# Sixteen idle matmuls before and inside the second norm of a decode block

## The chip, the cores and the metric

The kernel runs on one core of a Trainium2 chip, as one program. The metric is device time in microseconds (us) of one execution. The engines named below are PE (TensorE, the matrix engine; PEld is its weight load), DVE (VectorE), ACT (ScalarE), POOL (GpSimd) and SP (SyncE, whose queue issues nearly all transfers here). A matmul writes to PSUM, the accumulation memory, in banks of 512 columns.

## The reference

One transformer block in float32 for two sequences of one new token each: norm with a modulation from `c`, attention of 32 heads over a cache of 4096 keys and values, a second norm with modulation, and a dense layer pair with Mish between them.

```python
mod = (_silu(c) @ w_mod).reshape(c.shape[0], 6, 1, -1)
sa, ca, ga, sb, cb, gb = (mod[:, 0], mod[:, 1], mod[:, 2], mod[:, 3], mod[:, 4], mod[:, 5])
h = _layernorm(x, axis=-1) * (1 + ca) + sa
x = x + ga * _A_ref(h, A_k_cache, A_v_cache, A_wq, A_wo)   # softmax attention, 32 heads of 128
h = _layernorm(x, axis=-1) * (1 + cb) + sb
x = x + gb * _B_ref(h, B_w1, B_b1, B_w2)                   # 512 -> 1376, Mish, -> 512
```

Keys and values are 2 x 32 x 4096 x 128 floats each, so nearly everything that is read is cache: 297 MB in all, each byte used once.

## The kernel before, in words

All inputs are packed on the host into 36 loads, which go one after another through three rooms in SBUF (`load`, L142 to L155); a room is loaded again when what lay in it has been used (`used`, L159). SP issues the loads in their order and waits, ahead of a load, for the engine that still reads the room. The last load (m3 and w1, then m5 and w2: modulation 3, the first dense layer, a part of modulation 5, the second dense layer) is cut into seven transfers; its first waits for the end of head 30's V on PE, since the room it goes to held the values of heads 29 and 30.

Per head, DVE multiplies the keys by the query (L334) and sums (L337), PE brings the maxima together (L346), ACT takes the exponentials into `e_t` (L353), and PE multiplies them with the values: `weighted_v` (L371 to L382, the matmul is L375), 16 products of 512 columns for a head, each 32 columns of the array wide, four side by side. The program order of each engine is written by hand; nothing is moved by a scheduler.

After the last head's softmax comes the tail, where this change lies. In order on PE: V of heads 29 and 30 into the PSUM tile `ov[1]` (L488 to L490); the copy of it and its products with the denominators, `head_values` (L398, `otp`); `project_o` (L406, `att`); V of head 31 into `ov[0]` (L498); the folding of the attention output (L502, `xps`); `busy(1)`; head 31's `otp`; modulation 4 (L263) around the last head's output projection (L414). Then the second norm, `centred` and `rstd`: DVE sums, PE takes the mean over partitions (L226, `mean_b`), DVE subtracts and squares, PE takes the variance (L234, `var_b`), ACT and DVE make the reciprocal root. Modulation 3 (L263) waits for the last load's first piece; DVE joins both to `hq` (L543), PE turns it (L253, `h2ps`), DVE copies it to `h2t`, and the first dense layer follows (L554, `w1ps`, 16 products of up to 384 columns). Then Mish on ACT and DVE, and the second dense layer (L598, `yps`, 44 products), whose last products need the last pieces of the last load. Two sums on DVE and the store end the kernel.

Modulation 5 (`modulation_5`, L519 to L526, matmul L523) is put in pieces into gaps of this chain. Its first five terms have 20 rows each (`rows5`, padding to spread transfers), the next three 128 rows, the last 28; each term is four products of 128 columns, accumulated in `gps`, a part of `ov[0]`. `centred` takes a function `between` that is called after the squares and before the variance.

`busy(n)` (L310 to L314) computes nothing that is used: for `n` counts of 128 columns it multiplies the exponentials of another head with the unit matrix, 256 columns at a time, into `ov[1]`, which is free then. Such a product is called idle here.

## Time and profile before

| | |
|---|---|
| median of 3 runs | 697.68 us (697.03 to 698.01) |
| profiled execution | 696.76 us, its span 695.0 us |
| DVE busy | 588.2 us, 85% of the span |
| PE busy | 282.6 us, 41% |
| ACT busy | 44.2 us, 6% |
| HBM read | 297.17 MB, 428 GB/s over the span |
| load queue (q1) | 99.1% of 16 DMA engines |
| mean granted clock of TensorE | 0.671 |

The span runs from the first to the last instruction that the profiler recorded; the execution's time has a little around it. In the rows below, `L375` is a line of the kernel, `ov<-room,e` are the tiles written and read, `128*32` the rows and columns of the array that a matmul uses, `128x512` its output, `x32` a count. A matmul in float32 stands in the trace as two records, one per pass. In brackets stands how long the engine was idle ahead of it and what ended that. "PEclk" is the share of its full clock that TensorE was granted.

### The profile page before, as it was taken

Reading aid. Unit: us, or ns where it says so; the run is one execution under the profiler, and the core shown is the slowest. Engines: PE = TensorE matmul, PEld = TensorE weight load, DVE = VectorE, ACT = ScalarE, POOL = GpSimd, SP = SyncE. Lnnn points to the kernel's source line nnn. Section 1 sums busy time; section 2 is a strip of 40 time slices with the busy share of each in tenths; the row PEclk is TensorE's granted clock in tenths of the full one; section 3 lists DMA queues with packets and bytes.
Section 4 is the critical chain, followed back from the end, with each engine's and each line's share of the span. In section 5 each row is a group of like instructions: output and inputs, shape, how many; then the busy total and the mean of one; then the engine's idle time right before and its main releaser. Section 6 shows DMA issues by size and latency. Waiting matters only on the chain.

```text
span 695.0 us, 3978 instructions
## 1 busy us (share of the span) xinstructions
PE 282.6 (41%) x1664; PEld 102.0 (15%) x1664; DVE 588.2 (85%) x223; ACT 44.2 (6%) x169; POOL 4.4 (1%) x20
## 2 busy tenths in 40 slices
PE   2503334335145515335232705134343526124677
PEld 1201001001001201102100301011110101001235
DVE  3699899999999999999999989999999999899002
ACT  1000000000000000000000000000000010000011
POOL 2000000000000000000000000000000000000000
PEclk9755666668556665656585757666576657555789
DMA  9999999999999999999999999999999999999997
GB/s 378 464 426 422 423 445 453 420 426 430 422 457 434 427 430 427 438 441 427 426 441 426 450 426 426 430 435 438 438 426 424 445 430 446 426 421 425 429 419 303
DMA packets 6986, 297.49 MB, mean 428 GB/s; under 512 B 924, under 2 KB 1060, under 8 KB 1444
## 3 DMA queue, kind: packets, MB, share of 16 engines
q1 hardware_dynamic: 6808, 297.22, 99.1%
q8 instruction: 13, 0.21, 0.1%
q10 hardware_dynamic: 160, 0.02, 0.0%
q14 instruction: 5, 0.04, 0.0%
HBM read 297.17 MB, written 0.07 MB: 428 GB/s over the span
## 4 chain that ended last, share of the span: by engine, by line
DMA 67%; DVE 28%; PE 4%; issue 0%; ACT 0%; SPq 0%; DVEq 0%; ACTq 0%
DMA room<-in_load 67%; DVE room L334 14%; DVE s L337 14%; PE qps L307 1%; PE ov L375 1%; PE modps L263 1%; PE w1ps L554 1%; PE yps L598 0%; PE ov L523 0%; PE fps L569 0%; DVE m L350 0%; DVE hcw L296 0%; PE ov L314 0%; ACT q L308 0%; SPq L151 0%
## 5 line engine op out<-in xcount | busy, mean ns | idle before, releaser
L334 DVE TENSOR_TENSOR room<-room,q 128x8192 f32<-128x8192 f32 x32 | 278.1, 8692 | 46.4 <-DMA room<-in_load 40.3
L337 DVE TENSOR_REDUCE s<-room 128x64 f32<-128x8192 f32 x32 | 277.9, 8683 | 0.4 <-DVE m L350 0.3
L375 PE MATMUL ov<-room,e 128*32 128x512 f32 x1024 | 173.5, 829 | 77.2 <-ACT e L353 52.3
L346 PE MATMUL mt<-d,same 128*128 128x64 f32 x64 | 18.2, 379 | 199.7 <-DVE d L344 199.7
L375 PEld LDWEIGHTS ov<-room,e 128*32 128x32 f32 x1024 | 38.6, 143 | 183.2 <-issue 129.3
L353 ACT ACTIVATE e<-s,m 64x64 f32<-64x64 f32 x64 | 22.1, 345 | 554.2 <-DVE m L350 553.4
L346 PEld LDWEIGHTS mt<-d,same 128*128 128x128 f32 x64 | 13.1, 255 | 229.0 <-DVE d L344 182.0
L307 PE MATMUL qps<-room,hcw 128*128 128x512 f32 x64 | 44.4, 862 | 4.8 <-DMA room<-in_load 4.0
L361 PE MATMUL l<-l,ones 128*128 128x8 f32 x16 | 4.6, 358 | 75.4 <-ACT e L353 75.4
L398 PE MATMUL otp<-pick,o 128*128 128x8 f32 (+2 forms) x72 | 13.6, 316 | 33.6 <-ACT o L390 31.6
L307 PEld LDWEIGHTS qps<-room,hcw 128*128 128x128 f32 x64 | 17.1, 279 | 27.2 <-issue 21.3
L398 PEld LDWEIGHTS otp<-pick,o 128*128 128x128 f32 x72 | 12.8, 267 | 42.8 <-ACT o L390 39.8
L390 DVE COPY o<-ov 128x256 f32<-128x256 f32 x1 | 0.4, 425 | 21.8 <-ACT o L390 21.8
L361 PEld LDWEIGHTS l<-l,ones 128*128 128x128 f32 x16 | 3.8, 296 | 76.8 <-ACT e L353 76.8
L350 DVE TENSOR_REDUCE m<-mt 128x1 f32<-128x64 f32 x32 | 6.9, 217 | 7.6 <-PE mt L346 7.6
L406 PE MATMUL att<-room,ot 128*32 128x512 f32 x62 | 10.2, 719 | 5.2 <-DMA room<-in_load 4.7
L353 ACT ACTIVATION_READ_ACCUMULATOR e<-s,m 64x1 f32 x64 | 11.8, 185 | 0.0
L344 DVE TENSOR_SCALAR d<-half,m 128x64 f32<-128x64 f32 x32 | 8.1, 254 | 1.1
L342 DVE TENSOR_REDUCE m<-s 128x1 f32<-128x64 f32 x32 | 7.0, 217 | 0.9
L263 PE MATMUL modps<-room,ct 128*32 128x128 f32 (+1 forms) x128 | 6.8, 358 | 2.0 <-DMA room<-in_load 2.0
L390 ACT COPY o<-ov 128x512 f32<-128x512 f32 (+1 forms) x9 | 5.1, 561 | 25.4 <-PE ov L375 25.2
L308 ACT ACTIVATE q<-qps 128x512 f32<-128x512 f32 x8 | 4.8, 597 | 14.8 <-PE qps L307 14.6
(107 smaller groups left out, 63.1 us busy)
## 6 DMA issues: line engine op xcount, KB each, us to landing
room<-in_load SPq DMA_DIRECT2D x4, 4096.0 KB, 25.2
room<-in_load SPq DMA_DIRECT2D x1, 7168.0 KB
room<-in_load SPq DMA_DIRECT2D x1, 3072.0 KB, 26.1
room<-in_load SPq DMA_DIRECT2D x3, 1024.0 KB, 28.2
room<-in_load SPq DMA_DIRECT2D x1, 2400.0 KB, 13.1
room<-in_load SPq DMA_DIRECT2D x1, 1376.0 KB, 14.5
room<-in_load SPq DMA_DIRECT2D x1, 1280.0 KB, 15.1
room<-in_load SPq DMA_DIRECT2D x1, 768.0 KB
```

Of the source, the lines that this page charges most:

```text
L263: nc.tensor.matmul(ps[R * g : R * (g + 1)], lhsT=ct[:, k, :], rhs=t[:, k, :].rearrange("p (m n) -> p m n", m=n)[:, :, P * g : P * (g + 1)] ...
L307: nc.tensor.matmul(ps, lhsT=hcw[:, k, :], rhs=wq_t[ch][:, k, :], start=(k == 0), stop=(k == G - 1))
L334: nc.vector.tensor_tensor(out=k_t[h], in0=k_t[h], in1=qv, op=ALU.mult)
L337: nc.vector.tensor_reduce(out=s_t[h], in_=k_t[h], axis=AX.X, op=ALU.add)
L342: nc.vector.tensor_reduce(out=m_t[h][:, 0:1], in_=s_t[h], axis=AX.X, op=ALU.max)
L344: nc.vector.tensor_scalar(out=d, in0=half, scalar1=m_t[h][:, 0:1], scalar2=None, op0=ALU.mult)
L346: nc.tensor.matmul(mps[h], lhsT=same, rhs=d, start=True, stop=True)
L353: nc.scalar.activation(e_t[i][own_b, :, M * i + 4 * b : M * i + 4 * b + 4], s_t[h][own_b].rearrange("p (c m) -> p c m", m=4), AF.Exp, bias ...
L361: nc.tensor.matmul(lps[n], lhsT=ones, rhs=sum_t[n % 2], start=True, stop=True)
L375: nc.tensor.matmul(ov[bank][R * g : R * (g + 1), :], lhsT=e_t[h % HC][:, NB // 2 * part + c, :], rhs=v_t[h, part][:, c, :], start=(first a ...
L398: nc.tensor.matmul(tps[:, x], lhsT=o_t[m], rhs=pick_t[n][:, m, x], start=(m == 0), stop=(m == 3),)
L406: nc.tensor.matmul(att[R * i : R * (i + 1), :], lhsT=ot_t[n % 2][:, i, :], rhs=wo_t[n][:, i, :], start=(n == 0), stop=(n == H // HC - (2 i ...
```

## The change

`busy` gets the PSUM bank as an argument. Twelve idle products of 256 columns are put between head 29's V and head 30's, into `ov[0]`. In the second norm, two pieces of modulation 5 move ahead of the mean; three counts of idle columns (one product of 256, one of 128) take the place of the pieces between mean and variance; one idle product and two pieces follow modulation 3, where one piece stood; one idle product goes ahead of the last of these pieces, after `h2ps`. The sum of the pieces stays the same and so does their order among each other.

```diff
-    def busy(n):
+    def busy(n, bank=1):
...
-            nc.tensor.matmul(ov[1][:, :cols], lhsT=ident, ...
+            nc.tensor.matmul(ov[bank][:, :cols], lhsT=ident, ...
...
     for h in range(H - 3, H - 1):
+        if h == H - 2:
+            busy(24, 1 - N % 2)
         for part in range(2):
             weighted_v(h, part, N % 2, False, h == H - 2)
...
+    modulation_5(0, 2)
+
     xg = work.tile([P, P], F32, tag="sq", name="xg", bufs=1)
...
-    xc, var, rs = centred(x2, "b", add_x, lambda: modulation_5(0, 3))
+    xc, var, rs = centred(x2, "b", add_x, lambda: busy(3))
     mps3 = modulation("3", 1, wm3)
-    modulation_5(3, 4)
+    busy(1)
+    modulation_5(2, 4)
...
+    busy(1)
     modulation_5(4, PIECES)
```

PE's row before, from the sum of the denominators (`l`) to the end of head 30's V (`ov_110` is `ov[1]`, `ov_109` is `ov[0]`, `room_1196` holds the values of heads 29 and 30, `e_161` and `e_162` are their exponentials):

```order
L361 MATMUL l_1291<-l_167,ones 128x8 [waits PE_49,Activation_49]
L375 MATMUL ov_110<-room_1196,e_161 32x512 [waits DMAHW4_49]
L375 MATMUL ov_110<-room_1196,e_161 32x512 x15
L375 MATMUL ov_110<-room_1196,e_162 32x512 [waits DMAHW5_49]
L375 MATMUL ov_110<-room_1196,e_162 32x512 x15
```

And now:

```order
L361 MATMUL l_1291<-l_167,ones 128x8 [waits PE_49,Activation_49]
L375 MATMUL ov_110<-room_1196,e_161 32x512 [waits DMAHW4_49]
L375 MATMUL ov_110<-room_1196,e_161 32x512 x15
L314 MATMUL ov_109<-e_160,ident 128x256 x12
L375 MATMUL ov_110<-room_1196,e_162 32x512 [waits DMAHW5_49]
L375 MATMUL ov_110<-room_1196,e_162 32x512 x15
```

The twelve stand ahead of head 30's wait for its transfer and wait for nothing themselves.

PE's row in the second norm before (`modps_1386` is modulation 4, `modps_1434` modulation 3, `ct_104` the 20-row terms of modulation 5):

```order
L263 MATMUL modps_1386<-room_1227,ct 32x128 x8
L226 MATMUL mean_b<-rs_b,mean_w 128x1
L523 MATMUL ov_109<-room_1227,ct_104 32x128 x12
L234 MATMUL var_b<-rs_b,mean_w 128x1
L263 MATMUL modps_1434<-room_1344,ct 32x128 x16
L523 MATMUL ov_109<-room_1227,ct_104 32x128 x4
L253 MATMUL h2ps<-ident,hq 128x8
L523 MATMUL ov_109<-room_1227,ct_104 32x128 x4
```

And now (modulation 3 is `modps_1444`, its lines are up to six higher):

```order
L263 MATMUL modps_1398<-room_1227,ct 32x128 x8
L525 MATMUL ov_109<-room_1227,ct_104 32x128 x8
L226 MATMUL mean_b<-rs_b,mean_w 128x1
L314 MATMUL ov_110<-e_160,ident 128x256
L314 MATMUL ov_110<-e_160,ident 128x128
L234 MATMUL var_b<-rs_b,mean_w 128x1
L263 MATMUL modps_1444<-room_1356,ct 32x128 x16
L314 MATMUL ov_110<-e_160,ident 128x128
L525 MATMUL ov_109<-room_1227,ct_104 32x128 x8
L253 MATMUL h2ps<-ident,hq 128x8
L314 MATMUL ov_110<-e_160,ident 128x128
L525 MATMUL ov_109<-room_1227,ct_104 32x128 x4
```

Idle products that use all 128 rows now stand after the mean, after modulation 3 and after `h2ps`; two of the narrow pieces come ahead of the mean. The other engines' rows are the same as before.

More of the change, by code (lines that the diff above doesn't have):

```diff
@@ L308, in project_q @@
         nc.scalar.activation(q_t[ch].rearrange("p h d -> p (h d)"), ps, AF.Copy, scale=SCALE)
-    def busy(n):
+    def busy(n, bank=1):
         for lo in range(0, n, 2):
             cols = P * min(2, n - lo)
-            nc.tensor.matmul(ov[1][:, :cols], lhsT=ident, rhs=e_t[0].rearrange("p c m -> p (c m)")[:, :cols], start=True, stop=True)
+            nc.tensor.matmul(ov[bank][:, :cols], lhsT=ident, rhs=e_t[0].rearrange("p c m -> p (c m)")[:, :cols], start=True, stop=True)
     NB = NS // 4
```

## The prediction

> **What bounds the kernel now.** I read the page first, then the chain that ended last, then the windows of the tail, then its timeline and its DMA.

> ```profile
> span 695.0 us, 3978 instructions
> ...
> PEclk9755666668556665656585757666576657555789
> DMA  9999999999999999999999999999999999999997
> ...
> DMA 67%; DVE 28%; PE 4%; issue 0%; ACT 0%; SPq 0%; DVEq 0%; ACTq 0%
> ```

> The 16 DMA engines are full in every slice but the last. PE can move the time only where the chain leaves the transfers, in the last 15 us. The chain, in order of time (start, length, what):

> ```profile
> 623.99 37.76 DMA room<-in_load
> ...
> 661.78 5.37 PE ov L375 x32
> ...
> 667.17 13.12 DMA room<-in_load
> ...
> 680.34 1.12 PE modps L263 x32
> ...
> 682.34 0.58 PE ov L523 x8
> 682.92 4.15 PE w1ps L554 x16
> ...
> 690.18 2.61 PE yps L598 x88
> ```

> Head 30's V (L375) waits for its data until 661.75. The first piece of the last load is issued when it ends (667.17) and lands at 680.29. From there PE runs the chain: modulation 3, the first dense layer (w1ps, 4.15), the last one (yps), which ends at 692.79. The windows below are cut where the granted clock changes; columns are length, busy time of PE (instructions), PEld, DVE, ACT, POOL, then the clock, the DMA share and GB/s:

> ```profile
> 654.97:658.38 3.41, 1.29 (x13) 0.13 (x4) 0.00 (x0) 0.00 (x0) 0.00 (x0) 1.00 0.94 404
> 658.38:661.79 3.41, 0.01 (x1) 0.01 (x1) 0.00 (x0) 0.00 (x0) 0.00 (x0) 0.50 0.99 423
> 661.79:665.21 3.42, 3.42 (x18) 0.80 (x21) 0.00 (x0) 0.00 (x0) 0.00 (x0) 0.50 1.04 446
> ...
> 672.03:675.45 3.42, 2.13 (x25) 0.60 (x18) 0.00 (x0) 0.21 (x1) 0.00 (x0) 1.00 1.01 426
> ...
> 678.86:682.27 3.41, 2.69 (x68) 1.87 (x56) 1.51 (x8) 0.87 (x3) 0.00 (x0) 1.00 1.02 426
> 682.27:685.69 3.42, 3.42 (x31) 2.00 (x34) 0.17 (x1) 0.00 (x0) 0.00 (x0) 0.50 1.01 417
> ```

> Cut in steps of 3.41 us, each window has one clock, 1.00 or 0.50, which follows the window before. Head 30's V and the first dense layer both begin at 0.50. The first is explained by idleness (1.29 busy, 38%, then 0.50). The second is not: 2.69 of 3.41 busy (79%) is followed by 0.50, while 2.13 (62%) is followed by 1.00. The difference is what the products are. Of L523 alone (busy time and count of PE and PEld, clock, DMA):

> ```profile
> 678.86:682.27 3.41, 1.00 (x32) 0.47 (x20) 1.00 1.02 426
> ```

> 1.00 of the 2.69 us are modulation 5's pieces, which use 20 of the array's 128 rows. If they count for little, 1.69 us or less remain, and the two norm products of one column inside that count little too. So I take it that the gate weighs rows and columns, keeps full speed somewhere between 38% and 62% of a window of full-height work, and lost it here to the narrow pieces.

> [...]

> **The twelve products between head 29's V and head 30's.** Rows of the timeline:

> ```profile
> 652.62 3.64 PE L375 MATMUL ov<-room,e 128*32 128x512 f32 x32
> 653.50 0.13 PEld L375 LDWEIGHTS ov<-room,e 128*32 128x32 f32 x4 [0.30 <-issue]
> 653.93 0.13 PEld L375 LDWEIGHTS ov<-room,e 128*32 128x32 f32 x4 [0.30 <-issue]
> ...
> 662.64 0.20 PEld L375 LDWEIGHTS ov<-room,e 128*32 128x32 f32 x4 [0.66 <-issue]
> 663.50 0.20 PEld L375 LDWEIGHTS ov<-room,e 128*32 128x32 f32 x4 [0.65 <-issue]
> ...
> 667.17 0.35 SPq L151 DMA_DIRECT2D room<-in_load  x1
> ...
> 671.57 0.28 PEld L375 LDWEIGHTS ov<-room,e 128*32 128x32 f32 x8 [0.57 <-DMA room<-in_load]
> 674.05 0.16 PEld L375 LDWEIGHTS ov<-room,e 128*32 128x32 f32 x8 [2.20 <-DMA room<-in_load]
> ...
> room<-in_load SPq DMA_DIRECT2D x1, 2400.0 KB, 13.1
> room<-in_load SPq DMA_DIRECT2D x1, 1376.0 KB, 14.5
> ```

> One pass over 512 columns takes 0.43 us at clock 1.00 (653.50 to 653.93) and 0.86 at 0.50. The trace records two passes per product, so an idle one of 256 columns is 2 x 0.215 = 0.43 and twelve are 5.2 us. Head 29's V needs 8 passes, 652.62 + 3.44 = 656.1; the idle ones end at 661.3, before the data at 661.75. They wait for nothing, and at full clock they cost nothing. At half clock they would take 10.3 and end at 666.4; the row 654.97:658.38 is at 1.00 and they fill what was idle of it, so I take full.

> Head 30's V then starts at 1.00: 3.44 instead of 5.37, ending near 665.3, 1.9 earlier. Behind it wait ACT's copy, its products on PE, and on SP the last load's first piece. PE's gain is gone at once: head 31's V waits for data at 671.57 and 674.05 anyway. SP's issue comes 1.9 earlier into a full queue: DMA is busy at 0.94 and more in the rows above, and the piece (the two rows after the timeline: size and us to landing; 2400 KB are 5.8 us at 426 GB/s) lands at 680.29, so its bytes moved only from 674.5. I count 0; bounds 0 and, if the earlier issue fed a hole, 0.1.

> **The four idle products of the second norm** (five counts of 128 columns).

> ```profile
> 677.34 0.62 PE L263 MATMUL modps<-room,ct 128*32 128x128 f32 x16
> ...
> 678.27 0.38 PE L226 MATMUL mean_b<-rs_b,mean_w 128*128 128x1 f32 x2 [0.31 <-DVE x L533]
> ...
> 678.59 0.86 PE L523 MATMUL ov<-room,ct 20*32 20x128 f32 x24
> ...
> 679.43 0.30 PEld L234 LDWEIGHTS var_b<-rs_b,mean_w 128*128 128x128 f32 x2 [0.26 <-issue]
> ...
> 681.35 0.42 PE L523 MATMUL ov<-room,ct 20*32 20x128 f32 x8
> ...
> 681.95 0.39 PE L253 MATMUL h2ps<-ident,hq 128*128 128x8 f32 x2 [0.19 <-DVE hq L543]
> ...
> 682.38 0.17 DVE L545 COPY h2t<-h2ps 128x8 f32<-128x8 f32 x1 [0.48 <-PE h2ps L253]
> ...
> 669.06 6.24 SPq L151 DMA_DIRECT2D room<-in_load  x5
> ```

> A narrow piece streams 2 x 128 columns, 0.22 us (8 records are four products side by side, twice).
> - Two pieces go ahead of the mean: 0.44 us behind products ending at 677.8 to 677.96, so until 678.3 to 678.4; mean_b is 0 to 0.15 later.
> - Between mean and variance, 256 and 128 columns take 0.43 + 0.22 = 0.65 in place of three pieces (0.66): var_b does not move further. The variance has slack: hq waits for modulation 3, not for it.
> - After modulation 3 stand one idle product and two pieces, 0.22 + 0.44, in place of one piece, 0.22. PE is free at about 682.15, where h2ps could start at 681.95: +0.2.
> - After h2ps, 0.22 + 0.22 = 0.44 in place of 0.58 at half clock, beside the copy to h2t: −0.15.

> So the first dense layer starts where it did, within 0.2. Of its 4.15 us, 2.77 lie before 685.69 at 0.50; at 1.00 they are 1.39, so the layer takes 1.39 + 1.38 = 2.77, −1.4. Its second half needs the next piece (1376 KB; issued at 669.06) at 683.6, before 684.3. What follows keeps its length, and yps could start at 688.8.

> **What is late next.** The DMA's busy share in 40 slices of 688:695, 0.175 us each, and the store (size, us to landing):

> ```profile
> DMA  9978787878744543342213000000000000007500
> ...
> out<-y SPq DMA_DIRECT2D x1, 64.0 KB, 1.5
> ...
> 693.46 0.35 SPq L607 DMA_DIRECT2D out<-y  x1
> ```

> Weights arrive until 691.7 to 691.85. The store's bytes end between 694.5 and 694.65 and it lands at 693.46 + 1.5 = 694.96, a lag of 0.3 to 0.5. The last weights so land at 692.0 to 692.3, and their eight records need 0.42 (as at 681.35): yps ends at 692.4 to 692.75, against 692.79. The transfers nearly tie with PE's path already, and of 1.4 us 0.05 to 0.4 are left. Bounds: 0, and 0.75 if there were no lag and eight records took their share of yps, 0.24 (692.04). I take 0.1, near the long lag: the shares fall from slice to slice after 690, so single engines finish last, and the last one counts.

> **Sum.** The profiled execution took 696.76 (span 695.0 and 1.76 around it): 696.76 − 0 − 0.1 = 696.7. It is already the fastest shown; the runs' median is 697.68 (697.03 to 698.01), 0.92 more. I take that difference to be PE's path with the clock lost at a worse moment (the layer wholly at 0.50 takes up to 5.5, 1.4 more), which no row shows, and the change to remove it: 696.7 against 697.68, −0.14%. A measurement of this kernel can tell about 0.2% (1.4 us) from no change.

> **The rivals.**
> - *Nothing changes, 697.7.* Either the runs' scatter lies in the transfers, or the idle products of the norm do not hold the clock. For: transfers bound everything. Against: 79% lost the clock and 62% kept it, so the kind of product matters. [...]
> - *More than that, 696.1.* In executions with a late PE path the transfers end earlier than in this one, and the full 1.55 (1.4 + 0.15) comes off 697.68. For: the tie at 692.8 is one execution's. Against: the last bytes come at 691.8 here, and no row shows them earlier elsewhere.
> - *Slower, 699.8.* Head 30's V ends at 665.3, and until head 31's data PE has only four products of six columns and three of 512 side by side (two passes, 0.86 us), some 25% of a window, under the 38% that lost the clock above; then PE waits before 671.57 and 674.05 as well. A window lying there gives 0.50 to head 31's V (its last quarter, two passes, 0.9 later), modulation 3 (+1.1) and the dense layer (+1.0 against before): 696.76 + 3.0 = 699.8. It decides if the clock isn't back by 680. Against: the window of 62% holds the same waits for head 31's V and kept the clock, and idle products come again at 678.6.

> **How the numbers follow.** Forecast 0.50, nothing changes 0.18, more 0.14, slower 0.18. The forecast's own range is 696.0 (bound 0.75) to 697.4; 0.08 of it lies under 696.28. Faster by over 0.2%: 0.22; within: 0.61; slower: 0.17 (a part of that case ends inside the bound). The range 696.0 to 698.6 leaves out most of the slower case.

> **What would show it.** Right: L314 with 24 records between 656 and 661.4; V of head 30 about 3.5; clock 1.00 over the first dense layer and 2.7 for it; PE waiting for DMA inside yps. Wrong: a window of 0.50 after 668, w1ps above 4, or yps ending before the last bytes of 691.8 plus 0.4.

## The result and the profile after

| | before | after |
|---|---|---|
| median of 21 executions each, on the same chips | 698.31 us | 696.79 us |
| lowest to highest | 696.71 to 699.21 | 696.58 to 697.29 |
| ratio, 95% interval | | 0.9981 [0.9975, 0.9987] |

The changed kernel is 0.19% faster, clearly more than nothing and just inside the 0.2% that one measurement tells. The lowest times are nearly the same (696.71 and 696.58); what went is the scatter above them, 2.5 us before and 0.7 after. Two executions in the runs further down, one of the kernel before at 708.29 and one with the twelve alone at 782.70, lie far outside all others and are left out of the ratios.

The chain that ended last, after (start, length, what):

```profile
643.77 30.40 DMA room<-in_load
...
675.51 16.84 DMA room<-in_load
692.35 0.04 issue
692.39 0.47 PE yps L604 x8
692.86 0.03 issue
692.88 0.30 DVE y L611
```

No modulation, no first dense layer and no Mish stand in it any more. It runs from transfer to transfer (the dots stand for short pieces in which SP issues them); the last weights land at 692.35, eight records of the second dense layer follow, and the end is at 692.86, where it was before (692.79). In this profiled execution the change is worth nothing, as the profiled execution of before already tied with the transfers.

The windows of the tail, cut again in steps of 3.41 us, at whose edges the clock of the trace changes (columns as in the prediction; a "window" is such a step from here on):

```profile
652.86:656.27 3.41, 3.41 (x20) 0.87 (x16) 0.00 (x0) 0.00 (x0) 0.00 (x0) 0.50 0.99 425
656.27:659.68 3.41, 3.41 (x23) 2.18 (x16) 0.00 (x0) 0.00 (x0) 0.00 (x0) 1.00 0.90 387
...
676.75:680.16 3.41, 3.36 (x66) 2.66 (x65) 1.39 (x7) 0.44 (x2) 0.23 (x1) 1.00 0.97 409
680.16:683.58 3.42, 3.18 (x67) 2.31 (x70) 1.05 (x5) 0.87 (x3) 0.00 (x0) 1.00 1.00 421
683.58:686.99 3.41, 2.85 (x35) 1.66 (x27) 0.00 (x0) 0.58 (x3) 0.00 (x0) 1.00 1.00 411
```

The clock is 1.00 from 656.27 to the end, through the norm and the first dense layer. The windows lie elsewhere than before (boundaries at 676.75 and 680.16, before at 678.86 and 682.27). The timeline of the same stretch:

```profile
652.12 5.34 PE L375 MATMUL ov<-room,e 128*32 128x512 f32 x32 [0.49 <-DMA room<-in_load]
657.38 5.45 PE L314 MATMUL ov<-e,ident 128*128 128x256 f32 x24
662.76 3.64 PE L375 MATMUL ov<-room,e 128*32 128x512 f32 x32
...
674.21 1.07 PE L375 MATMUL ov<-room,e 128*32 128x512 f32 x8 [1.48 <-DMA room<-in_load]
...
678.62 0.38 PE L226 MATMUL mean_b<-rs_b,mean_w 128*128 128x1 f32 x2
...
682.40 0.39 PE L253 MATMUL h2ps<-ident,hq 128*128 128x8 f32 x2
...
683.39 2.78 PE L560 MATMUL w1ps<-room,h2t 128*32 128x384 f32 x32
...
691.13 1.08 PE L604 MATMUL yps<-room,actt 128*32 128x128 f32 x32 [0.34 <-DMA room<-in_load]
692.39 0.43 PE L604 MATMUL yps<-room,actt 128*32 128x128 f32 x8 [0.17 <-DMA room<-in_load]
```

The first dense layer takes 2.78 instead of 4.15, and PE now waits twice for weights inside the second (0.34 and 0.17).

### The profile page after: what moved, and what is told of

Read it like the earlier page. It is cut to its first block, busy times and chain, and to the rows that moved or that the text cites. A ratio compares the mean times of both kernels' runs of the same rounds, so it can differ in the third digit from the quotient of the medians.

```text
span 695.1 us, 4042 instructions
## 1 busy us (share of the span) xinstructions
PE 290.5 (42%) x1696; PEld 109.5 (16%) x1696; DVE 588.2 (85%) x223; ACT 44.2 (6%) x169; POOL 4.4 (1%) x20
## 2 busy tenths in 40 slices
DMA  9999999999999999999999999999999999999997
## 4 chain that ended last, share of the span: by engine, by line
DMA 67%; DVE 30%; PE 2%; SPq 0%; issue 0%; ACT 0%; DVEq 0%
DMA room<-in_load 67%; DVE room L334 15%; DVE s L337 15%; PE qps L307 1%; PE modps L263 1%; SPq L151 0%; DVE m L350 0%; DVE hcw L296 0%; PE hps L253 0%; ACT q L308 0%; PE yps L604 0%; DVE y L611 0%; DVE hq L287 0%; DVE hq L286 0%; DVE y L612 0%
## 5 line engine op out<-in xcount | busy, mean ns | idle before, releaser
L375 PE MATMUL ov<-room,e 128*32 128x512 f32 x1024 | 170.6, 820 | 69.3 <-ACT e L353 39.8
L375 PEld LDWEIGHTS ov<-room,e 128*32 128x32 f32 x1024 | 38.4, 143 | 173.6 <-issue 125.2
L307 PE MATMUL qps<-room,hcw 128*128 128x512 f32 x64 | 46.8, 902 | 4.4 <-DMA room<-in_load 3.6
L314 PE MATMUL ov<-e,ident 128*128 128x256 f32 (+1 forms) x36 | 8.5, 372 | 0.0
L263 PE MATMUL modps<-room,ct 128*32 128x128 f32 (+1 forms) x128 | 7.0, 364 | 1.4 <-DMA room<-in_load 1.4
## 6 DMA issues: line engine op xcount, KB each, us to landing
room<-in_load SPq DMA_DIRECT2D x1, 1376.0 KB, 14.5
```

What stands on the lines that cost most here:

```text
L263: nc.tensor.matmul(ps[R * g : R * (g + 1)], lhsT=ct[:, k, :], rhs=t[:, k, :].rearrange("p (m n) -> p m n", m=n)[:, :, P * g : P * (g + 1)] ...
L307: nc.tensor.matmul(ps, lhsT=hcw[:, k, :], rhs=wq_t[ch][:, k, :], start=(k == 0), stop=(k == G - 1))
L314: nc.tensor.matmul(ov[bank][:, :cols], lhsT=ident, rhs=e_t[0].rearrange("p c m -> p (c m)")[:, :cols], start=True, stop=True)
L375: nc.tensor.matmul(ov[bank][R * g : R * (g + 1), :], lhsT=e_t[h % HC][:, NB // 2 * part + c, :], rhs=v_t[h, part][:, c, :], start=(first a ...
```

## The experiments

The theory: the granted clock follows full-height streaming (products that use all 128 rows of the array); the norm's idle products keep the clock up over the first dense layer, and then the last load's bytes set the end. The rivals: the twelve products between the values carry the gain; the new places of the pieces do; any busy PE would do; or before's scatter lies in the transfers. Medians are given, and the ratio to the kernel before on the same chip with its 95% interval. That ratio is not the quotient of the two medians; where a few executions lie apart, the two differ. The medians of before are 698.35 (33 executions) for the first four runs, 698.26 (19) for the two on which idle products are needed, and 698.56 (31) for the last four.

### The two halves apart

The change without the twelve:

```diff
-        if h == H - 2:
-            busy(24, 1 - N % 2)
```

> The change's second half alone: pieces moved and four idle products in the second norm, the twelve left out. Theory (the norm's full-height idle products hold the clock over the first dense layer, and the last load's bytes then set the end): 696.7 to 697.0, as the whole change, and yps ends on a wait for DMA. Rival (the twelve idle products carry the gain): 698.0 to 698.5, as before.

Measured: 696.93 (696.52 to 697.19, 11 executions), ratio 0.9985 [0.9976, 0.9995]. It ends as the whole change does:

```profile
675.66 16.78 DMA room<-in_load
692.44 0.04 issue
692.48 0.47 PE yps L602 x8
```

The kernel before with only the twelve:

```diff
-    def busy(n):
+    def busy(n, bank=1):
...
+        if h == H - 2:
+            busy(24, 1 - N % 2)
```

> The change's first half alone: twelve idle products between the V of heads 29 and 30, the second norm as before. Theory: no gain, since head 31's V waits for its data anyway and the norm still loses the clock: 698.0 to 698.7. Rival (they carry the gain): 696.7 to 697.0. Rival (their end leaves a hole that loses the clock for the tail): 699 or more.

Measured: 697.95, just under the range expected, ratio 1.0003 [0.9989, 1.0018]: no gain and no loss in the ratio. One execution took 701.64, and no trace shows why. The windows of the trace (an execution of 697.82) show the hole that the slower rival spoke of, and that it costs nothing there:

```profile
666.25:669.66 3.41, 2.45 (x26) 1.32 (x22) 0.00 (x0) 0.75 (x2) 0.00 (x0) 1.00 0.97 406
669.66:673.08 3.42, 3.42 (x23) 1.46 (x19) 0.00 (x0) 0.58 (x1) 0.00 (x0) 0.50 1.08 450
...
676.49:679.90 3.41, 3.08 (x73) 2.54 (x72) 1.39 (x7) 0.44 (x2) 0.42 (x1) 1.00 0.95 404
679.90:683.32 3.42, 3.37 (x44) 2.40 (x44) 0.88 (x4) 0.87 (x3) 0.00 (x0) 0.50 1.01 423
```

Head 30's V ended at 666.76, the clock was lost at 669.66, and head 31's V, slow now, filled the window and won it back before its last data. Then the norm lost it again at 679.90, as before. The chain shows what that costs:

```profile
680.39 1.94 PE modps L263 x32
...
684.04 4.11 PE w1ps L556 x16
...
691.26 2.59 PE yps L600 x88
```

The norm is that of the kernel before, whose profiled execution lost the clock 2.4 us later, at 682.27. Here modulation 3 takes 1.94 instead of 1.12 and the dense layer hardly changes (4.11 against 4.15); PE ends at 693.85 instead of 692.79 and the execution takes 697.82 instead of 696.76, 1.06 more in both. So the whole gain is the norm's half. Whether the twelve add the 0.14 us between 696.79 and 696.93 can't be told: the two ranges overlap.

### The places without the idle products

Pieces of modulation 5 where the change puts them, `busy` in no place of the norm, and not the twelve (against the kernel before):

```diff
+    modulation_5(0, 2)
...
-    xc, var, rs = centred(x2, "b", add_x, lambda: modulation_5(0, 3))
+    xc, var, rs = centred(x2, "b", add_x, None)
     mps3 = modulation("3", 1, wm3)
-    modulation_5(3, 4)
+    modulation_5(2, 4)
```

> The second norm with modulation 5's pieces where the change puts them, without any idle product, and without the twelve. Theory (the clock matters, not the places): 698.0 to 699.0, with 0.50 in the window of the first dense layer. Rival (the new places shorten PE's path): 697.0 or less.

Measured: 699.50, ratio 1.0016 [1.0001, 1.0031] (before on the same chip: 698.35). That is 0.5 above the 698.0 to 699.0 expected, a miss on the slower side. The chain shows why:

```profile
681.68 1.86 PE modps L263 x32
683.54 1.01 PE ov L523 x16
684.55 0.53 PE h2ps L253 x2
685.08 0.58 PE ov L523 x8
685.66 4.06 PE w1ps L556 x16
```

The clock was lost at 681.41, so modulation 3 took 1.86 instead of 1.08, and the pieces behind it, two where one stood, are ahead of `h2ps` on the path at half speed (1.01). So the new places lengthen PE's path when the clock is lost. Whether they are of use when it is held is not shown: no run has the idle products with the pieces in their old places. Three of the twelve executions were at 696.7 to 696.9, where, by the theory, no window lay badly; no trace of one of them was taken.

### Does a busy PE suffice, or must it use the rows?

The norm's half, with its four idle products on 20 rows (against the changed kernel, without the twelve):

```diff
+    def busy20(n):
...
+            r20 = slice(ROW0, ROW0 + ROWS)
+            nc.tensor.matmul(ov[1][:, :cols], lhsT=ident[r20, :], rhs=e_t[0].rearrange("p c m -> p (c m)")[r20, :cols], start=True, stop=True)
...
-    xc, var, rs = centred(x2, "b", add_x, lambda: busy(3))
+    xc, var, rs = centred(x2, "b", add_x, lambda: busy20(3))
     mps3 = modulation("3", 1, wm3)
-    busy(1)
+    busy20(1)
...
-    busy(1)
+    busy20(1)
```

> As the norm's half alone, but the four idle products multiply 20 rows in place of 128 and stream as many columns in as much time. Theory (the clock gate weighs rows): as without idle products, 698.0 to 699.0. Rival (any streaming product counts): 696.7 to 697.0.

Measured: 700.38, ratio 1.0029 [1.0016, 1.0043]. The same number of instructions, the same columns, and 3.5 us more than with 128 rows. The direction is the theory's; the size is a miss, 1.4 above the 699.0 that was expected at most: at half speed the idle products stand on PE's path themselves (1.12, 0.72 and 0.72 us in its chain). Its windows (here PE is busy without a gap):

```profile
676.08:679.49 3.41, 3.41 (x68) 2.95 (x68) 1.16 (x6) 0.44 (x2) 0.42 (x1) 1.00 0.98 412
679.49:682.90 3.41, 3.41 (x39) 2.61 (x38) 1.18 (x7) 0.86 (x3) 0.00 (x0) 0.50 1.02 429
682.90:686.32 3.42, 3.42 (x34) 2.06 (x37) 0.31 (x2) 0.00 (x0) 0.00 (x0) 0.50 1.00 413
686.32:689.73 3.41, 3.41 (x27) 2.11 (x22) 0.00 (x0) 0.00 (x0) 0.00 (x0) 0.50 0.91 369
```

A window that is busy from end to end is followed by 0.50, and another one by 0.50 again. Busy time is refuted as the measure. The matmul records carry their rows, columns and length. Count each pass as its streaming time at full clock (0.43 us for 512 columns), times rows/128, times columns of the array/128: then the first three windows hold 0.35, 0.27 and 0.07 of their length. The last section sets such shares against the clock in all traces.

### Which of the norm's idle products are needed

Both from the change without the twelve, so with the pieces moved. Only the two products between mean and variance:

```diff
     mps3 = modulation("3", 1, wm3)
-    busy(1)
     modulation_5(2, 4)
...
-    busy(1)
     modulation_5(4, PIECES)
```

> The norm's half with only the idle products between mean and variance (256 and 128 columns), without the one after modulation 3 and the one after h2ps. Theory (the clock is lost where a window of 3.41 us holds under some 0.37 of full-height streaming): most windows over the norm are now above it, only those that start after the idle products and end before the dense layer is under way fall under: median 696.8 to 697.1, one execution in six or so at 698 or more. Rival (the share counts over a longer time, or all four are needed): median 698 or more.

Measured: 696.87 (696.60 to 697.24, 11 executions), ratio 0.9980 [0.9971, 0.9988]. Two products of sixteen, with the moved pieces, bring the whole gain. The one loss in six or so that was expected did not come in eleven executions. Its windows over the norm hold 0.50 and 0.43 by the count above, and the clock stays:

```profile
676.97:680.38 3.41, 3.41 (x69) 2.92 (x68) 1.16 (x8) 0.44 (x2) 0.42 (x1) 1.00 0.98 414
680.38:683.79 3.41, 3.36 (x71) 2.38 (x73) 1.33 (x8) 0.87 (x3) 0.00 (x0) 1.00 1.01 423
```

The other way round, only the two late ones:

```diff
-    xc, var, rs = centred(x2, "b", add_x, lambda: busy(3))
+    xc, var, rs = centred(x2, "b", add_x, None)
```

> The norm's half with only the two idle products of 128 columns after modulation 3 and after h2ps. Theory: windows that start between the last products of modulation 4 and the mean still hold only modulation 3 and 0.2 to 0.4 us of idle products, 0.31 to 0.37, and lose the clock: two executions in five or more at 698 to 700, median above 697.1. Rival (any full-height product near the dense layer suffices): 696.7 to 697.0.

Measured: 700.82, ratio 1.0027 [1.0010, 1.0043]; seven of eight executions at 699 or more. The direction was as the theory had it, the size was worse than expected. In its trace the clock is lost at 680.28 and stays lost for three windows:

```profile
680.28:683.70 3.42, 3.06 (x36) 2.38 (x36) 1.30 (x7) 0.87 (x3) 0.00 (x0) 0.50 0.99 416
683.70:687.11 3.41, 3.41 (x37) 2.11 (x40) 0.17 (x1) 0.00 (x0) 0.00 (x0) 0.50 1.01 415
687.11:690.52 3.41, 3.41 (x29) 2.11 (x23) 0.00 (x0) 0.00 (x0) 0.00 (x0) 0.50 0.79 320
```

What stands on the path at half clock (idle products and moved pieces among it) delays the dense layer to 686.52, so that it fills no window before the third.

### Who sets the end: PE's path or the bytes

Two of the four slices of 128 inputs that the first dense layer adds up (k-steps) are left out, in either kernel; what follows then works on half of the sum:

```diff
-    for k in range(G):
+    for k in range(2):
...
-                stop=(k == G - 1),
+                stop=(k == 1),
```

> The changed kernel with two of the first dense layer's four k-steps left out (8 of 16 products, about 1.3 us of PE's path at full clock; its weights are still loaded). Theory (after the change the last load's bytes set the end): no change, 696.6 to 697.0. Rival (PE's path still sets it): 695.5.

Measured: 696.75, with one of ten executions at 701.82 that no trace explains; the other nine lie between 696.62 and 696.93. Some 1.3 us of PE work less, and no time: the transfers set the end.

> The kernel before with the same two k-steps left out (2.1 to 2.6 us at half clock). Theory (before, PE's path lies behind the transfers by a different amount in each execution): 696.7 to 697.1 with a narrow scatter, as the changed kernel. Rival (the scatter of before lies in the transfers): 698.0 or more, or as wide a scatter.

Measured: 697.41, ratio 1.0001 [0.9985, 1.0017]: not the 696.7 to 697.1 expected. Seven of ten executions lie between 696.86 and 697.50, the other three at 699.8 to 700.5, above all 31 of the kernel before on that chip (to 699.20). So the median falls by 1.15 and the ratio sees no gain. Its chain:

```profile
681.30 1.86 PE modps L263 x32
...
684.85 2.76 PE w1ps L554 x10
...
690.72 2.58 PE yps L598 x88
```

Here the clock was lost at 681.28, ahead of modulation 3. Even with half a layer, at half clock, PE's path ends at 693.30, some 0.4 us behind the 692.8 to 692.9 at which the transfers let the changed kernel end. The step taken out was not the only one that the lost clock stretches: what was expected left out modulation 3 and the pieces. That the three executions near 700 had the second dense layer at half clock too (half a layer leaves less streaming to win it back with) is argued, not shown.

The last two transfers (512 KB) and the eight products that need them left out:

```diff
             take(t[:, lo:], keys)
+            if ("w2", 0) in keys:
+                srcs = srcs[:-2]
...
-    for n in range(NCH):
+    for n in range(NCH - 2):
...
-                stop=(n == NCH - 1),
+                stop=(n == NCH - 3),
```

> The changed kernel without the last two transfers of the last load (2 x 256 KB, about 1.2 us of DMA) and without the eight products of the second dense layer that need them. Theory (bytes set the end): 695.9, since the third from last transfer then lands at 691.1 and three groups of four products follow it. Rival (PE's path sets it): 696.4, by the 0.44 us of products alone.

Measured: 696.01 (expected 695.9), ratio 0.9974 [0.9964, 0.9984]. The end moves with the bytes:

```profile
674.71 16.17 DMA room<-in_load
690.88 0.04 issue
690.92 0.91 PE yps L606 x24
```

> The kernel before without the same two transfers and eight products. Theory (PE's path sets the end in most executions): 697.9, faster than before by the 0.44 us of the products, not by the 1.2 of the transfers. Rival (bytes set it): 697.2 or less.

Measured: 697.96, ratio 0.9993 [0.9981, 1.0005], as expected 697.9 for a kernel that PE's path ends. Its first dense layer took 4.07, and the last one waited for no transfer:

```profile
684.06 4.07 PE w1ps L556 x16
...
691.24 2.15 PE yps L600 x72
```

Together, on this chip: without the two transfers the changed kernel ends at 696.01, where with half a layer it ended at 696.75. The old one falls by 0.6 in the medians (698.56 to 697.96), near the 0.44 that its eight products are worth, and by its interval perhaps by nothing. Taking PE work away helps the changed kernel by nothing and lowers the old one's median by 1.15. So the bytes end the changed kernel, and, by these medians, PE's path ends most executions of the old one.

## Why the prediction was right, step by step

Forecast 696.7, measured 696.79; "within 0.2%" had the largest chance, and the ratio is 0.9981.

- *The clock was lost to narrow pieces, and full-height products hold it.* Right, and now shown: 20 rows instead of 128 turn 696.9 into 700.4. The share that kept full speed, taken to lie between 38% and 62% of a window, is near 0.37 by the count of the last section, at the lower edge; the window of the trace before that was 79% busy and lost the clock (678.86 to 682.27) holds 0.29. The four idle products are more than needed; the two between mean and variance do it.
- *The dense layer: 2.77 instead of 4.15.* Measured 2.78.
- *The twelve cost nothing and bring nothing.* Right as a sum, wrong in a part. The prediction took full clock for them and an end at 661.3. In the trace after, a window of 0.50 fell on head 29's V (652.86 to 656.27), they ran from 657.38 to 662.8, past the arrival of head 30's data (661.75 in the trace before), and V ended at 666.5, 0.7 earlier than before instead of 1.9. The cover named for it, head 31's wait for its data until 674, took all of it either way.
- *The dense layer starts where it did, within 0.2.* Mis-sized: 683.39 against 682.85, 0.54 later. `mean_b` came 0.35 later, of which 0.16 was head 31's last data (674.21 against 674.05), but that costs nothing, as `hq` waits for modulation 3 and came only 0.07 later. `h2ps` came 0.45 later, held up on PE: the idle product after modulation 3 keeps the next piece off for 0.42 (681.41 to 681.83), the two pieces keep `h2ps` off for 0.57, and 0.22 and 0.44 had been counted, their streaming alone. The idle product behind `h2ps` did not win 0.15 but lost another 0.1: it starts 0.24 after `h2ps`, and the piece behind it 0.40 after that. Each of these products has weight loads of its own in the trace, which are not in the sum; that they are what is missing is likely, not shown. The last dense layer so could start at 689.27, not 688.8; PE still had to wait for weights in it.
- *The transfers are late next, and keep all but 0.1.* Right: the gain in the profiled execution is nil (692.86 against 692.79). The last weights landed at 692.35, just past the 692.0 to 692.3 taken, with a lag from the last bytes of 0.5, the long end.
- *The runs' 0.92 above the profiled execution is PE's path with the clock lost at a worse moment.* This was chosen, with no row for it, and the forecast of a faster median rests on it. That the windows lie elsewhere in another execution had no row either; the traces show boundaries at 678.86 (before), 676.75 (after) and 677.87 (before with half of the layer). The trace with the twelve alone now has such a case: the clock lost at 679.90, the end 1.06 later. The scatter of 2.5 us that becomes 0.7 speaks for it too, and leaving out bytes or PE work on either side shows where each kernel ends. The way there was another than the one named: the layer did not go from 4.15 towards 5.5 but took 4.11, and modulation 3 and the pieces grew. No execution of the kernel before itself that took longer was traced. The kernel before with half of the layer (697.41) fits it only with modulation 3 and the pieces counted in.
- *The slower rival.* Its mechanism exists: the hole after head 30's V lost the clock in the trace with only the twelve, and in the changed kernel's traces with half a layer (at 669.71) and with fewer bytes (at 669.44). Its price was not paid: the clock was back at 673.08, 673.12 and 672.85, and none of 21 executions of the changed kernel was above 697.29. The two idle products of the norm guard the rest. The executions of 701.64 and 701.82, both of kernels with the twelve, have no trace, so a rare loss of this kind is not excluded.

## What to carry to other kernels

Look at the clock in slices as long as its steps (3.41 us here) before pricing a short chain of matmuls: here a window 79% busy with small products was followed by half speed for the layer behind it (4.15 us instead of 2.78), and so was one that was busy from end to end with narrow idle products among them (the layer took 4.57). A few full-height idle products where PE waits anyway, here two of 0.65 us together, held the clock (696.87); narrow ones (700.38), or late ones alone (700.82), did not hold it here and lengthened the path. And ask which wait is next: here the transfers end the kernel where PE's path ends it in a good execution (692.86 and 692.79), so the change could only cut the scatter.

## What the runs showed of the hardware

| | before: windows, share | after: windows, share | all twelve traces: windows, share |
|---|---|---|---|
| full speed kept | 29, 0.38 or more | 35, 0.37 or more | 369, 0.35 or more |
| full speed lost | 34, 0.37 or less | 29, 0.35 or less | 394, 0.37 or less |
| half speed ended | 34, 0.41 or more | 29, 0.37 or more | 392, 0.34 or more |
| half speed stayed | 100, 0.37 or less | 102, 0.37 or less | 1215, 0.37 or less |

With 0.37 as the divide in both directions, eleven windows of the 2370 fall on the wrong side, all with shares of 0.34 to 0.37. So in these traces holding the clock and winning it back went with the same share. At half clock a pass took twice as long (0.86 us for 512 columns), so by this count a window there has to stream for 0.74 of its time to hold 0.37; that is an estimate from the two numbers.

The rows belong in the count: in the seven traces in which the norm lost the clock (before, and with the twelve alone, the moved pieces alone, narrow idle products, late ones alone, half a layer before, fewer bytes before), its window holds 0.29 to 0.35 with them, and 0.44 to 0.54, well over 0.37, without. In the trace before it is 0.29 and 0.46. In the traces with full-height idle products between mean and variance the norm's windows hold 0.41 to 0.52 (in the trace after 0.52 and 0.44), and the clock stays. All of this is a fit to float32 products of one kernel and its variants, and says nothing of others.
